# Moving value products, projections and squares by a step or two in a fused attention and feed-forward kernel

## Chip, cores and metric

The kernel runs on one core of one Trainium2 chip, in one launch. The metric is the device time of that launch in microseconds (us). A core has TensorE (PE, with its weight loads shown as PEld), VectorE (DVE), ScalarE (ACT), GpSimd (POOL), and SyncE (SP), which issues the DMAs here. Each engine executes its own instructions in order and waits on semaphores.

## What is computed

A pre-normalized attention block and a gated feed-forward, both with a residual, on 2048 tokens of width 512 with 32 heads of 16:

```python
def _A_ref(x, wqkv, wo):                       # S=2048, D=512, H=32, Dh=16
    qkv = (x @ wqkv).reshape(B, S, 3, H, Dh).transpose(2, 0, 3, 1, 4)
    q, k, v = qkv[0], qkv[1], qkv[2]
    p = _softmax(jnp.einsum("bhqd,bhkd->bhqk", q, k) * (Dh ** -0.5), axis=-1)
    o = jnp.einsum("bhqk,bhkd->bhqd", p, v)
    return o.transpose(0, 2, 1, 3).reshape(B, S, D) @ wo

def _B_ref(x, w_gate, w_up, w_down):           # F=1792
    return (_gelu(x @ w_gate) * (x @ w_up)) @ w_down

h = x + _A_ref(_layernorm(x), A_wqkv, A_wo)
h2 = h + _B_ref(_layernorm(h), B_w_gate, B_w_up, B_w_down)
```

Inputs and output are bfloat16. There is no causal mask; the softmax subtracts the maximum of each row.

## The kernel before

**Units and steps.** The 2048 queries are cut into 8 groups of 256, and the 32 heads into 8 slots of 4. One (group, slot) is a unit; there are 64, in the order of the groups. The main loop (`while True`, L1403) runs in steps (`tick`); a unit has 16 steps.

**First pass.** In a step TensorE computes two 128x512 score tiles (`p1_pair`, L825) and VectorE takes their row maxima in one instruction (`p1_consume`, L840). After 16 steps GpSimd combines the maxima of the unit (`negm_part`, `negm_pre`), writes them with corrections into `ST`, SP transposes `ST` into `STG`, and GpSimd adds that to the query tile (L888), so that the second pass subtracts the maximum inside the matmul.

**Second pass.** It runs `P2_START` = 24 steps behind the first. In a step TensorE computes two transposed score tiles (`p2_tile`, L904) and ScalarE turns each into probabilities (`p2_consume`, L933), which go to a ring of 34 tiles in `PTM`, `PTE` and `PTG`.

**Eleven joint units.** In the units of `JOINT` one step of the first pass is left out (step 14). Two differences of score tiles (`item_diff`, L1022 and L1024 on TensorE, L1027 on ScalarE) are made ahead, and VectorE folds them in at step 10 or 11 (L837). ScalarE makes up its two tiles in the steps that follow.

**Dense work.** Everything else on TensorE is done in items, generators that give out a piece per step: projections of queries, keys and values, value products (`item_pv`, L947, 64 products of a unit in four pieces), the output projection (`item_oproj`, L1087 and L1091), gate and up products (`item_gate`, `item_up`, L1168), down products (`item_down`, L1220). `Dense.piece` holds three lists: `prio` (value products and output projections, ordered by the step before which they may not start), `extra` (differences) and `ready` (all else). An item of `ready` starts only if it ends before the next item of `prio` may start. Steps without a piece get dummy products (`dummy`, L1380). The dense item and the second pass share four PSUM banks.

**Account of ScalarE.** `act_lag` estimates how far ScalarE is behind: an exponential adds 0.478, an eviction 0.48, a step takes off 1.135. Gate and up products start only at a lag of at most `LAG_START` = 0.3, squares are written at a lag of at most `LAG_OP` = 0.2, tanh at `LAG_TH`, differences at `LAG_EXTRA`; otherwise they are put off by a step (`defer`). A difference is forced from the second step of its own unit.

**The chain behind a value product.** When the four pieces are done, ScalarE evicts the sum to `OB` (L669). SP transposes it to `OBT` (`o_turn`, L973). Five steps later GpSimd gets the reciprocal (L981) and the scaling into `Otok` (L985). When all 8 slots of a group are there, `post_onT` loads the residual (`load_xres`, L1060) and transposes `Otok` into `OnT` (L1067), through `clear`, which lets such a transfer out only at certain steps of a unit. It then adds the two output projections to `prio`. After a projection, ScalarE evicts with a sum (L1094), then squares with a sum (`sq`, L1101); GpSimd normalizes (L1111 to L1125), and `post_hnT` transposes into `hnT_l` (L1077, again through `clear`). Some steps after the second of these, `add_ffn_when` adds the group's feed-forward to `ready`: 7 gate and 7 up items and 2 down items, with a chain of multiplications on GpSimd and a tanh on ScalarE (L1148) for each gate item.

**The tail.** After the last maximum the second pass goes on alone for 24 steps with wide exponentials (L921), VectorE evicts in ScalarE's place (L658), and the feed-forward of the last group follows.

Of the kernel before, what the change touches and what calls it, by code (L numbers as in the profile page):

```python
# [218 lines left out]

NPT_M, NPT_E, NPT_G = 23, 4, 7  # L220
NPT = NPT_M + NPT_E + NPT_G
PV_T = (13, 14, 16, 17)
ADDX = 3
LAGX = 8
PAUSE = 1
# [4 lines left out]
LAG_OP = 0.2  # L230
# [1 line left out]
SLOPE = 0.02  # L232
JOINT = (12, 14, 17, 20, 25, 28, 33, 36, 41, 44, 49)
J_AT, J_GONE = 10, 14
LAG_EXTRA = 0.2
POLY = 1.3
TICK = 1.135
TOOK = {1.04: 1.13, 0.62: 0.7, 1.27: 1.26, 1.45: 1.67, 0.31: 0.4}
# [3 lines left out]
def bass_sequential_preLN__mha_block__geglu_ffn__prompt_kernel(nc, A_x, A_wqkv, A_wo, B_x, B_w_gate, B_w_up, B_w_down, out):  # L242
    dbg = None
    with ExitStack() as es:
# [279 lines left out]
        class Dense:  # L524
# [27 lines left out]
            def piece(self):  # L552
                if self.single and self.pause > 0:
                    return 0
                while True:
                    if self.gen is None:
# [6 lines left out]
                        elif self.prio and (not self.single or self.prio[0][3] <= self.now):  # L563
                            self._start(self.prio.pop(0))
                        elif self.extra and not tight() and act_lag[0] <= LAG_EXTRA and self.now + 2 <= lim and not (self.ready and self.ready[0][0] is item_up):
                            self._start(self.extra.pop(0))
# [26 lines left out]
        dense = Dense()  # L593
        behind = [0]
        def tight():
            return dense.now // 16 in JOINT and dense.now % 16 >= J_GONE - 2 or bool(behind[0])

        deferred = []
        def defer(k, fn):
            deferred.append((dense.now + k, fn))  # L600
        force = [False]
# [47 lines left out]
        act_lag = [0.0]  # L649
        def act_more(cost):  # L650
            act_lag[0] += cost
# [4 lines left out]
        def evac_act(o_ap, i_ap, reads, writes, scale=None, extra=(), bias=None, then=None, cost=0.48):  # L656
            if dve_free[0] and scale is None and bias is None:
                P.op("dve", lambda e: e.tensor_copy(out=o_ap, in_=i_ap), reads=reads, writes=writes, extra_deps=extra)  # L658
                if then is not None:
                    then()  # L660
                return
            act_more(cost)
            kw = {}
            if scale is not None:
                kw["scale"] = scale
            if bias is not None:
                P.op("act", lambda e: e.activation(out=o_ap, in_=i_ap, func=ACT.Identity, bias=bias, **kw), reads=list(reads) + ["kbias"], writes=writes, extra_deps=extra)
            else:
                P.op("act", lambda e: e.activation(out=o_ap, in_=i_ap, func=ACT.Copy, **kw), reads=reads, writes=writes, extra_deps=extra)  # L669
            if then is not None:  # L670
                then()
# [264 lines left out]
        def item_pv(b, ui):  # L936

            gi, slot = units[ui]
            for p in range(4):
                while not force[0] and dense.now < P2_START + 16 * ui + 4 * p + 5:  # L940
                    yield ("wait", 1)
                for m in (2 * p, 2 * p + 1):
                    for i in range(2):
                        kt = 2 * m + i
                        for g in range(4):
                            pi = pt_of[(ui, m, g)]
                            P.op("pe", lambda e, g=g, kt=kt, pi=pi, i=i: e.matmul(pbank[32 * g:32 * g + 17, b, 0:256], VA[:, kt, 4 * slot + g, :],  # L947
                                                                                  PTt(pi)[:, 256 * i:256 * i + 256], start=(kt == 0), stop=(kt == NT - 1), tile_position=(0, 32 * g)),
                                 reads=[("V", kt), "VA_ones", ("PT", pi)], writes=[("pb", b)], sig=(g == 3 and i == 1))
                    for g in range(4):  # L950
                        pt_busy.discard(pt_of.pop((ui, m, g)))
                if p < 3:
                    yield 2
            par, col = slot // 2 % 2, slot % 2
            if gi == GL and slot >= NSLOT - 2:
                evac_act(OA[:, par, 256 * col:256 * col + 256], pbank[:, b, 0:256], [("pb", b)], [("OA", par, col), ("RB", 1)], cost=0.27)
                if col == 0:
                    dense.add(item_ofin, gi, front=True, est=3, not_before=dense.now + 3)
            else:
                evac_act(OB[:, ui % 2, :], pbank[:, b, 0:256], [("pb", b)], [("OB", ui % 2)], cost=0.27, then=lambda: o_turn(ui))  # L960
            pv_done.add(ui)
            return 2

        pv_done = set()
        P2_START = 16 + LAGX

        ob_busy = {}
        def o_turn(ui):
            gi, slot = units[ui]
            par = ui % 2  # L970
            assert not ob_busy.get(par), "GpSimd too far behind"
            ob_busy[par] = True
            P.dma("sp", lambda e: e.dma_start_transpose(out=OBT[:, par, :, :], in_=OB[:, par, :]), ("obT", par), reads=[("OB", par)], writes=[("OBT", par)])  # L973
            o4 = OBT[:, par].rearrange("p q (g i) -> p q g i", i=32)
            defer(5, lambda: o_norm(gi, slot, par, o4, ("OBT", par), ob_busy))
# [25 lines left out]
            yield  # L1001

        def clear(fn):
            if not force[0] and not 5 <= dense.now % 16 <= 14:
                defer(1, lambda: clear(fn))
            else:
                fn()
# [36 lines left out]
        def add_ffn(gi):  # L1044
            for f in range(NFC // 2):
                dense.add(item_gate, gi, f, est=3)
                dense.add(item_up, gi, f, est=3)
            for k in range(2):
                dense.add(item_down, gi, k, est=5)

        def add_ffn_when(gi):
            if w_pieces or not qkv_over[0]:
                defer(1, lambda: add_ffn_when(gi))
            else:
                add_ffn(gi)

        def load_xres(gi):
            assert gi < 2 or ffn_done.get(gi - 2), "dense stream too far behind (residual reuse)"
            for k in range(2):
                P.dma("sp", lambda e, k=k: e.dma_start(out=g_h(gi, k), in_=xv[:, 2 * gi + k, :]), ("xres", gi % 2, k), writes=[("h", gi % 2, k)])  # L1060

        otok_consumed = {}
        def post_onT(gi, k):
            gp = gi % 2
            if k == 0:
                load_xres(gi)
            P.dma("sp", lambda e: e.dma_start_transpose(out=OnT[:, k, :, :], in_=Otok[:, k, :]),  # L1067
                  ("onT", k), reads=[("Otok", s_) for s_ in range(NSLOT)], writes=[("OH", k)])
            if k == 1:
                otok_consumed[gi] = True  # L1070
            dense.add(item_oproj, gi, k, front=True, est=3, not_before=dense.now + 4)

        hn_left = {}
        ffn_done = {}
        def post_hnT(gi, k):
            gp = gi % 2
            P.dma("sp", lambda e: e.dma_start_transpose(out=hnT_l[gp][:, :, 128 * k:128 * k + 128], in_=hn_sb[:, k, :]),  # L1077
                  ("hnT", 2 * gp + k), reads=[("OH", k)], writes=[("hnT", gp, k)])
            hn_left[gi] = hn_left.get(gi, 2) - 1
            if hn_left[gi] == 0:  # L1080
                defer(3, lambda: add_ffn_when(gi))

        def item_oproj(b, gi, k):
            gp, t = gi % 2, 2 * gi + k
            hh = g_h(gi, k)
            for hc in range(4):
                P.op("pe", lambda e, hc=hc: e.matmul(pbank[:, b, :], OnT[:, k, hc, :], wo_sb[:, hc, :], start=(hc == 0), stop=False),  # L1087
                     reads=[("OH", k), "wo"], writes=[("pb", b)], sig=False)
                if hc == 1:
                    yield 2  # L1090
            P.op("pe", lambda e: e.matmul(pbank[:, b, :], ident[:], hh, start=False, stop=True),  # L1091
                 reads=["ident", ("h", gp, k)], writes=[("pb", b)], sig=True)
            act_more(0.48)
            P.op("act", lambda e: e.activation(out=hh, in_=pbank[:, b, :], func=ACT.Copy, accum_out=hsum[:, t:t + 1]),  # L1094
                 reads=[("pb", b)], writes=[("h", gp, k), ("hsum", t)])
            def sq():
                if not force[0] and act_lag[0] > LAG_OP:
                    defer(1, sq)
                    return
                act_more(0.48)  # L1100
                P.op("act", lambda e: e.activation(out=hn_sb[:, k, :], in_=hh, func=ACT.Square, accum_out=hsq[:, t:t + 1]),  # L1101
                     reads=[("h", gp, k)], writes=[("OH", k), ("hsq", t)])
                defer(1, lambda: pool.add(ln2_from_sums(gi, k, t), then=lambda: defer(2, lambda: clear(lambda: post_hnT(gi, k)))))
            defer(2, sq)
            return 3
# [297 lines left out]
        while True:  # L1403
# [71 lines left out]
            if p2_ok and t2 % 16 == 0:  # L1475
                dense.add(item_pv, t2 // 16, front=True, est=5, not_before=tick + PV_T[0])
            if doubles[0]:
# [61 lines left out]
```

## Time and profile before

| | |
|---|---|
| median of 3 runs | 1240.03 us (1239.23 to 1241.87) |
| profiled execution | 1240.23 us, span 1238.5 us |
| VectorE busy | 1182.2 us (95%) |
| ScalarE busy | 1196.3 us (97%) |
| TensorE busy | 1099.2 us (89%), of it 206.0 us dummies (L1380) |
| GpSimd busy | 785.3 us (63%) |
| row maxima L840 | 1002, 1141.9 us |
| first maximum starts, last one ends | 14.73 us, 1183.08 us |
| squares L1101 | 14 |
| transposes OnT<-Otok, hnT_l<-OnT | 14 each, 2.7 and 2.6 us to landing in the median |
| granted TensorE clock | full, but for two spells of 3.4 us at half (from 820.4 and 1090.1 us) |

Times within the profile count from the start of the span. A row of a group names line, engine and operation, what is written and read, the count, then busy time and the mean of one in ns, then the idle time of that engine just before the group and what ended it. A row of a timeline has start, duration, engine, line, operation and count, and in brackets the idle time before it. A row of a stretch has its bounds, its length, the busy time (and number of instructions) of PE, PEld, DVE, ACT and POOL, the granted TensorE clock, the share of the DMA engines and GB/s.

### The profile page before, as it was taken

The numbers are of one execution on the slowest core, as the hardware profiler recorded it, in microseconds if no ns is written. First come the engines' busy times: TensorE is split into PE (matmuls) and PEld (weight loads), VectorE is DVE, ScalarE is ACT, GpSimd is POOL, SyncE is SP. The second block draws the span as 40 slices with busy tenths as digits, with TensorE's granted clock in tenths as the row PEclk, the third lists the DMA queues.
The fourth block names the chain that finished last, engine by engine and source line by source line (L and its number), as shares of the span: only waits on it lengthen the run. The fifth ranks groups of instructions, "written<-read, shape, count | busy, mean of one in ns | idle before, by whom it ended". The sixth has DMA issues, their size and how long they took to land.

```text
span 1238.5 us, 31200 instructions
## 1 busy us (share of the span) xinstructions
PE 1099.2 (89%) x12389; PEld 429.3 (35%) x12588; DVE 1182.2 (95%) x1111; ACT 1196.3 (97%) x2433; POOL 785.3 (63%) x1624
## 2 busy tenths in 40 slices
PE   7898888888888999889988999989988898888888
PEld 3232222233333333333333333333333333323345
DVE  8999999999999999999999999999999999999933
ACT  7899999999999999999999999999999999999992
POOL 8555884455756467674667638574676847865781
PEclk9999999999999999999999999999999999999999
DMA  5111113400010001000010100100001000010000
GB/s 151 27 30 25 30 27 108 117 10 8 10 25 17 14 12 23 16 15 17 8 27 12 14 17 8 27 16 15 12 10 30 12 18 8 7 32 20 8 15 18
DMA packets 68656, 31.52 MB, mean 25 GB/s; under 512 B 53920, under 2 KB 67488, under 8 KB 68512
## 3 DMA queue, kind: packets, MB, share of 16 engines
q1 hardware_dynamic: 68512, 29.52, 9.9%
q8 instruction: 101, 1.65, 0.6%
q14 instruction: 43, 0.35, 0.1%
HBM read 11.80 MB, written 2.10 MB: 11 GB/s over the span
## 4 chain that ended last, share of the span: by engine, by line
ACT 59%; DVE 30%; PE 8%; issue 1%; POOL 1%; DMA 1%
ACT PTM L933 33%; DVE PM L840 29%; ACT PTG L933 10%; ACT PTE L933 6%; PE pbank L1220 2%; ACT th_sb L1148 2%; ACT u_sb L669 2%; ACT g_sb L669 1%; PE pbank L825 1%; ACT PTM L921 1%; PE pbank L904 1%; PE pbank L1380 1%; PE pbank L1168 1%; ACT OB L669 1%; ACT OnT L1101 1%
## 5 line engine op out<-in xcount | busy, mean ns | idle before, releaser
L840 DVE TENSOR_REDUCE PM<-pbank 128x2 f32<-128x1024 f32 x1002 | 1141.9, 1213 | 11.3 <-PE pbank L904 7.4
L933 ACT ACTIVATE PTM<-pbank 128x512 bf16<-128x512 f32 x1357 | 727.4, 704 | 6.6 <-PE pbank L904 2.0
L904 PE MATMUL pbank<-QT,KT 32*128 32x256 bf16 x4096 | 517.6, 273 | 17.8 <-ACT PTM L933 6.5
L825 PE MATMUL pbank<-KT,QT 32*128 32x512 bf16 x2026 | 390.5, 384 | 25.3 <-DVE PM L840 10.7
L1380 PE MATMUL pbank<-ones_bf,ident 128*128 128x512 bf16 x639 | 206.0, 384 | 65.0 <-ACT PTM L933 31.9
L933 ACT ACTIVATE PTG<-pbank 128x512 bf16<-128x512 f32 x407 | 227.6, 704 | 1.2
L825 PEld LDWEIGHTS pbank<-KT,QT 32*128 32x128 bf16 x2026 | 98.7, 91 | 367.6 <-DVE PM L840 134.4
L904 PEld LDWEIGHTS pbank<-QT,KT 32*128 32x128 bf16 x4096 | 171.5, 92 | 90.4 <-ACT PTM L933 47.2
L933 ACT ACTIVATE PTE<-pbank 128x512 bf16<-128x512 f32 x236 | 137.3, 700 | 0.6
L947 PE MATMUL pbank<-PTM,VA 128*17 128x256 bf16 x2776 | 126.0, 274 | 5.2 <-ACT PTG L933 1.1
L981 POOL TENSOR_TENSOR LINV<-OBT,negone 128x8 f32<-128x8 bf16 x62 | 103.4, 1667 | 0.0
L1380 PEld LDWEIGHTS pbank<-ones_bf,ident 128*128 128x128 bf16 x804 | 46.2, 97 | 137.4 <-ACT PTM L933 90.8
L947 PEld LDWEIGHTS pbank<-PTM,VA 128*17 128x17 bf16 x2776 | 59.9, 89 | 49.7 <-issue 29.8
L1158 POOL TENSOR_TENSOR th_sb<-g_sb 128x512 f32<-128x512 f32 x49 | 50.9, 1039 | 34.9 <-ACT g_sb L669 34.9
L868 POOL TENSOR_TENSOR MX<-PM,MX 128x8 f32<-128x8 f32 x64 | 12.8, 200 | 92.7 <-DVE PM L840 92.1
L1168 PE MATMUL pbank<-hnT_l,wg_sb 128*128 128x256 bf16 x448 | 66.6, 274 | 2.8 <-ACT PTG L933 0.2
L1168 PE MATMUL pbank<-hnT_l,wu_sb 128*128 128x256 bf16 x448 | 66.5, 275 | 2.8 <-ACT PTM L933 0.2
L888 POOL TENSOR_TENSOR QT<-QT,STG 128x256 bf16<-128x256 bf16 x64 | 42.7, 668 | 35.0 <-DMA STG<-ST 35.0
L1157 POOL TENSOR_TENSOR th_sb<-th_sb,g_sb 128x512 f32<-128x512 f32 x49 | 62.1, 1267 | 3.2
L1160 POOL TENSOR_TENSOR th_sb<-th_sb,g_sb 128x512 f32<-128x512 f32 x49 | 62.1, 1267 | 2.9
L1212 POOL TENSOR_TENSOR GUT<-th_sb,u_sb 128x512 bf16<-128x512 f32 x49 | 62.1, 1267 | 2.0
L855 POOL TENSOR_TENSOR MX<-PM,MX 128x8 f32<-128x8 f32 x64 | 12.9, 201 | 74.8 <-DVE PM L840 74.0
(164 smaller groups left out, 1138.6 us busy)
## 6 DMA issues: line engine op xcount, KB each, us to landing
QKS<-QKS SPq DMA_DIRECT2D x27, 112.0 KB, 2.1
x_sb<-in_A_x_dram SPq DMA_DIRECT2D x4, 512.0 KB, 5.6
xres<-in_A_x_dram SPq DMA_DIRECT2D x16, 128.0 KB, 2.3
out_dram<-out_sb SPq DMA_DIRECT2D x16, 128.0 KB, 1.7
wg_sb<-in_B_w_gate_dram SPq DMA_DIRECT2D x4, 448.0 KB, 4.0
wu_sb<-in_B_w_up_dram SPq DMA_DIRECT2D x4, 448.0 KB, 3.9
wd_sb<-in_B_w_down_dram SPq DMA_DIRECT2D x3, 512.0 KB, 5.0
STG<-ST SPq DMA_TRANSPOSE x64, 2.3
```

Source lines behind the costliest of these rows:

```text
L825: P.op("pe", lambda e, g=g, b=b: e.matmul(pbank[:, b, :], QT[32 * g:32 * g + 32, c, slot, 128 * qt:128 * qt + 128], KT[32 * g:32 * g + 32, ...
L840: P.op("dve", lambda e: e.tensor_reduce(out=PM[:, par, qt, kc, g:g + 2], in_=pbank[:, b:b + 2, :], axis=AX.X, op=ALU.max), reads=[("pb", b ...
L904: P.op("pe", lambda e, kt=kt, i=i: e.matmul(pbank[:, b, 256 * i:256 * i + 256], KT[32 * g:32 * g + 32, slot, 128 * kt:128 * kt + 128], QT[ ...
L933: P.op("act", lambda e, b=b, pi=pi: e.activation(out=PTt(pi), in_=pbank[:, b, :], func=ACT.Exp), reads=[("pb", b)], writes=[("PT", pi)], e ...
L947: P.op("pe", lambda e, g=g, kt=kt, pi=pi, i=i: e.matmul(pbank[32 * g:32 * g + 17, b, 0:256], VA[:, kt, 4 * slot + g, :], PTt(pi)[:, 256 * ...
L981: P.op("pool", lambda e: e.tensor_tensor(out=li, in0=o4[:, :, :, 16], in1=negone[:, 0:8].rearrange("p (q h) -> p q h", q=2), op=ALU.pow), ...
L1157: o(1.27, lambda e: e.tensor_tensor(out=ts_, in0=ts_, in1=gs, op=ALU.mult), [("th", par), ("g", par)])], then=done)
L1158: pool.add([o(1.04, lambda e: e.tensor_tensor(out=ts_, in0=gs, in1=gs, op=ALU.mult), [("g", par)], dE), o(0.62, lambda e: e.tensor_scalar( ...
L1160: o(1.27, lambda e: e.tensor_tensor(out=ts_, in0=ts_, in1=gs, op=ALU.mult), [("th", par), ("g", par)])], then=poly_done)
L1168: P.op("pe", lambda e, dc=dc, fc=fc, i=i: e.matmul(pbank[:, b, 256 * i:256 * i + 256], w[:, dc, 128 * fc:128 * fc + 128], hT[:, dc, :], st ...
L1212: P.op("pool", lambda e: e.tensor_tensor(out=o_ap, in0=shp(ts_), in1=shp(us), op=ALU.mult), reads=[("th", par), ("u", par)], writes=o_keys ...
L1380: P.op("pe", lambda e: e.matmul(pbank[:, b, :], ident[:], ones_bf[:, 0:512], start=True, stop=True), reads=["ident", "ones_bf"], writes=[( ...
```

## The change

Six places of the order are changed; no computation is.

- The four pieces of a unit's value products may start at steps 15, 16, 17 and 18 after the unit's second pass began. Before, the first could start at step 13 and the loop's own condition was 4p + 5 for piece p.
- A difference may be taken early at a lag of 0.3 instead of 0.2.
- `clear` lets transfers out at steps 5 to 13 of a unit instead of 5 to 14.
- The output projection starts at the earliest 5 steps behind its transfer instead of 4.
- The feed-forward is added 4 steps behind its second transfer instead of 3.
- A square counts 0.48 more lag while a gate or up product is running.

```diff
-PV_T = (13, 14, 16, 17)
+PV_T = (15, 16, 17, 18)
...
-LAG_EXTRA = 0.2
+LAG_EXTRA = 0.3
...
             for p in range(4):
-                while not force[0] and dense.now < P2_START + 16 * ui + 4 * p + 5:
+                while not force[0] and dense.now < P2_START + 16 * ui + PV_T[p]:
                     yield ("wait", 1)
...
         def clear(fn):
-            if not force[0] and not 5 <= dense.now % 16 <= 14:
+            if not force[0] and not 5 <= dense.now % 16 <= 13:
                 defer(1, lambda: clear(fn))
...
-            dense.add(item_oproj, gi, k, front=True, est=3, not_before=dense.now + 4)
+            dense.add(item_oproj, gi, k, front=True, est=3, not_before=dense.now + 5)
...
             if hn_left[gi] == 0:
-                defer(3, lambda: add_ffn_when(gi))
+                defer(4, lambda: add_ffn_when(gi))
...
             def sq():
-                if not force[0] and act_lag[0] > LAG_OP:
+                if not force[0] and act_lag[0] + (0.48 if dense.gen is not None and dense.cur in (item_gate, item_up) else 0) > LAG_OP:
                     defer(1, sq)
                     return
```

The main loop, which the diff does not touch, adds a unit's value products with `not_before=tick + PV_T[0]` (L1476).

## The prediction

> **What bounds the kernel now.** I read the page first (busy times, chain, costliest groups), then the waits of VectorE, then the timeline of ScalarE and VectorE around the waits, then of TensorE and the DMA queue, then busy times by stretch.
>
> ```profile
> span 1238.5 us, 31200 instructions
> ...
> PE 1099.2 (89%) x12389; PEld 429.3 (35%) x12588; DVE 1182.2 (95%) x1111; ACT 1196.3 (97%) x2433; POOL 785.3 (63%) x1624
> ...
> ACT 59%; DVE 30%; PE 8%; issue 1%; POOL 1%; DMA 1%
> ...
> L840 DVE TENSOR_REDUCE PM<-pbank 128x2 f32<-128x1024 f32 x1002 | 1141.9, 1213 | 11.3 <-PE pbank L904 7.4
> ```
>
> The row maxima (L840) set the length: 1002 of them fill 1141.9 of 1238.5 us with only 11.3 us of idle before them. What the change can win in the main stage is what VectorE idles there:
>
> ```profile
> DVE PM L840 <- PE pbank L904: 7.4, 23, 1.1
> ```
>
> One maximum lasts 1.21 us, but 16 undisturbed ones start within 18.10 us, 1.13 apart, so every gap also loses an overlap of 0.08: 7.4 + 23 x 0.08 = 9.2 us is the ceiling. All 23 waits are for TensorE, which executes in order and is itself held up by ScalarE (no free bank) or by a DMA. ScalarE's view:
>
> ```profile
> 815.86 0.82 ACT L1101 ACTIVATE OnT<-xres 128x512 bf16<-128x512 bf16 x1
> 816.38 0.39 ACT L1101 ACTIVATION_READ_ACCUMULATOR OnT<-xres 128x1 f32 x1
> 816.47 1.27 ACT L933 ACTIVATE PTM<-pbank 128x512 bf16<-128x512 f32 x2
> 817.42 0.81 ACT L669 ACTIVATE u_sb<-pbank 128x512 f32<-128x512 f32 x1
> 817.90 2.29 ACT L933 ACTIVATE PTM<-pbank 128x512 bf16<-128x512 f32 x4
> 819.80 0.88 ACT L1027 ACTIVATE OA<-pbank 128x512 f32<-128x512 f32 x1
> ```
>
> From start to start an exponential or an eviction takes 0.48 us, a square (L1101 with its accumulator read) 0.61. A step of 1.13 needs two exponentials, 0.96, so only 0.17 to 0.18 us per step is left for all else. Here a square, an eviction and a difference (1.57 us) fall into four steps that hold 0.7. VectorE just behind:
>
> ```profile
> 818.77 2.35 DVE L840 TENSOR_REDUCE PM<-pbank 128x2 f32<-128x1024 f32 x2 [0.20 <-PE pbank L904]
> 821.72 1.22 DVE L840 TENSOR_REDUCE PM<-pbank 128x2 f32<-128x1024 f32 x1 [0.60 <-PE pbank L904]
> 823.23 3.56 DVE L840 TENSOR_REDUCE PM<-pbank 128x2 f32<-128x1024 f32 x3 [0.29 <-PE pbank L904]
> ```
>
> The other large wait is a transposing transfer that an output projection waits for. It goes out behind another transpose and the residual load:
>
> ```profile
> 1082.86 1.17 SPq L973 DMA_TRANSPOSE OBT<-OB  x1
> 1084.08 1.05 SPq L1060 DMA_DIRECT2D xres<-in_A_x_dram  x2
> 1085.17 3.38 SPq L1067 DMA_TRANSPOSE OnT<-Otok  x2
> ```
>
> ```profile
> 1088.53 0.60 PE L1087 MATMUL pbank<-wo_sb,OnT 128*128 128x512 bf16 x2 [1.75 <-DMA OnT<-Otok]
> ```
>
> Behind it TensorE runs at half clock for 3.4 us, as it does at 820.4:
>
> ```profile
> 820.43:823.85 3.42, 3.09 (x31) 0.82 (x30) 2.53 (x3) 2.89 (x7) 2.32 (x7) 0.50 0.09 19
> ...
> 1086.70:1090.10 3.40, 1.65 (x15) 0.45 (x11) 2.33 (x3) 2.09 (x6) 2.51 (x6) 1.00 0.39 80
> 1090.10:1093.50 3.40, 3.40 (x18) 0.74 (x17) 2.99 (x3) 3.16 (x8) 2.24 (x8) 0.50 0.01 2
> ```
>
> **Part by part.** No instruction is added or removed; all is order. The sum goes against the profiled execution's own 1240.23 us (span 1238.5 and 1.7 around it); the median of the runs, 1240.03, is 0.2 lower.
>
> *Squares.* Of the 14 squares, five share a step with a running gate or up product in the order of before: those at 525.44, 670.65, 815.86, 946.39 and 958.19. Each is followed 1.56 us later by the eviction of that product. Idle of VectorE behind them: 0.21, 0.21, 0.20 + 0.60 + 0.29, 0.46, 0.17: 2.14 us in seven gaps, and 7 x 0.08 = 0.56 of lost overlap, 2.7 together. The new condition adds 0.48 to the account of ScalarE's lag while such a product runs, so a square stays back until there is room. It is not lost: 0.61 us is worked off in steps whose account is empty. What it delays is normalization on GpSimd and the transpose into hnT_l; in all four groups concerned the feed-forward of the group before still runs for some 35 to 43 steps, so nobody waits for that. I take 2.3 of the 2.7, since the difference behind three of them (L1027, forced at the second step of its unit) stays unless the larger LAG_EXTRA places it earlier. Bounds: +0.5 (a held square meets another activation) to -2.7.
>
> *Projection one step later.* Only one of the 14 transfers was waited for. It cost VectorE 1.07, then 0.34 and 0.46 at half clock: 1.87, with three overlaps 2.1. One step is 1.13 of TensorE's 1.75 us wait. But the value products end one step later as well, and their eviction and transpose (L973) stand ahead of this transfer on the queue: if they stay ahead, transfer and projection move together and nothing is gained. If the transfer goes out first, as in the other groups, all of 2.1 goes. Bounds 0 to -2.1; I take -1.4, nearer to the second, because six groups of seven stand that way.
>
> *Value products at 15, 16, 17, 18 of their unit instead of 13, 14, 15, 17* (the old loop's condition 4p+5 binds only the last). Four pieces without the empty step between: dense work gets one more step in sixteen. TensorE pays nothing, since a piece of 16 products replaces dummies of the same 0.43 us; the covering dummies are L1380's 206 us. On TensorE's queue the pieces stand behind the exponentials that they read; one or two steps more relieve waits of L947 (5.2, 1.6 and 0.7 us of idle by operand), which lie only partly on the path. Probability tiles are freed up to two steps later: the ring of 34 refills the first of them at step 17, products at 15, so ScalarE does not wait. The eviction (OB) and its transpose go out one step later; SP waits there for ScalarE, and what stands behind it on SP is at most an OnT or hnT_l transpose and, six steps on, STG. GpSimd's reciprocal runs at the unit's end in both orders, with one step less of cover; its queue idles 35.0 us before L888 as it is. Estimate from the gaps of 0.17 to 0.33 that recur beside these products (486 to 526 us): -0.5, bounds -2.3 to +2.3, as they may vanish or double.
>
> *Window 5 to 13 and feed-forward 4 steps behind.* No transpose of before goes out at step 14, and no gate product waits for its transfer: 0. For the last group the delays add up to two or three steps, 2.3 to 3.4 us, before its feed-forward; its last up product ends at 1201.9 while the last value products begin at 1202.64, and these move two short steps of 0.92 as well: 0, bounds 0 to +2.1 (two groups of 1.05 on TensorE behind the loop).
>
> *Tail.* Two of the last four pieces move behind the last exponentials. TensorE has 0.25 + 0.72 idle there and a piece is 0.43: +0.2, bounds 0 to +0.9.
>
> Sum: -2.3 - 1.4 - 0.5 + 0 + 0.2 = -4.0: 1236.2 for the profiled execution, 1236.0 for the median.
>
> The clock enters two of these terms. The half-clock spell follows a window of 3.4 us in which TensorE was busy 1.65 us, with no single gap above 1.75; before 820.43 the gaps were shorter still. So here a light window is enough, and with the waits the spells should go: the -4.0 counts on that.
>
> The Trainium skill (TensorE: Matmul & The Clock Gate, "Why this matters for your kernels") asks for no idle gap above about 3 us if the clock is not to drop; by that rule neither of these waits causes its spell, the spells would stay, and the sum would be -2.0 instead.
>
> **Rivals.**
> 1. *ScalarE overfilled (slower).* With one more step for dense work a unit can carry four gate, up or projection evictions instead of three. A unit with at most six activations beside its exponentials takes 18.10 us; those of 488 to 507 and 507 to 526 with seven and eight take 18.89 and 18.76. At 0.7 each, twelve more such units cost 8.4: 1236.0 + 8.4 = 1244.4. It decides from the seventh activation on, and from more than six such units the kernel is slower. Against: the planner charges 0.478 per exponential and 0.48 per eviction, as measured, and starts no gate or up product above a lag of 0.3.
> 2. *Only reshuffled: the change doesn't do what it says.* The held squares and differences meet other activations, and the transfer still goes behind L973. With +0.5 and 0 in place of -2.3 and -1.4 the sum is +0.2: 1240.2. For: the projection's transfer and the value products move by the same step.
> 3. *Half-clock spells recur.* If two windows stay light, their part stays: 0.60 + 0.29 + 0.34 + 0.46 and four overlaps, 2.0: 1238.0. For: the window before 820.4 has no long wait in it. Against: all other windows of the main stage keep full clock.
> The rule of the Trainium skill quoted above gives this time too.
> 4. *The repeated gaps go too.* With feed-forward further ahead at each group's boundary most of the ceiling of 9.2 is won: 1232. For: the gaps near 497, 505 and 516 return in three groups. Against: nothing in the change aims at them.
> 5. *Tail.* The last gate and up fall behind the last value products: 2.1 more on the path, 1238.1.
>
> **How the numbers follow.** Forecast 0.42, rival 1 0.15, rival 2 0.13, rival 3 0.08, rival 4 0.16, rival 5 0.06. A measurement here can tell 0.2%, 2.5 us, from no change. Faster by more than that (below 1237.6): forecast, rival 4, and half of 3 and 5, 0.65. Same: 2 and the other halves, 0.20. Slower (above 1242.5): 0.15. The range goes from 1230, just beyond the ceiling, to 1243.5, into rival 1; the forecast's own is 1233.5 to 1238.
>
> **What would show it.** Right: no square within two microseconds ahead of an eviction of g_sb or u_sb; VectorE's waits for L904 down from 7.4 to about 4.5 us; no wait of L1087 for OnT; OBT's transposes one step later against the maxima. Wrong: L840's idle at or above 11.3, units of 18.7 us and more in greater number, half-clock spells at new places, or more than 55.4 us behind the last maximum.

## Result and the profile after

The changed kernel takes 1234.78 us in the median of five runs (1234.71 to 1235.26) against 1240.03: a ratio of 0.9954, 95% interval 0.9943 to 0.9966. The forecast was 1236.0. The profiled execution takes 1234.76 us (span 1232.9).

Of the page of the changed kernel, the span, the busy times and the group of the row maxima:

```profile
span 1232.9 us, 31298 instructions
...
PE 1102.3 (89%) x12444; PEld 427.4 (35%) x12580; DVE 1179.1 (96%) x1107; ACT 1195.2 (97%) x2437; POOL 784.4 (64%) x1624
...
L840 DVE TENSOR_REDUCE PM<-pbank 128x2 f32<-128x1024 f32 x1002 | 1141.4, 1213 | 8.8 <-PE pbank L904 5.1
```

The maxima do the same work in the same time, with 2.5 us less idle before them. In the waits of VectorE (total, times, longest):

```profile
DVE PM L840 <- PE pbank L904: 5.1, 20, 0.4
```

The longest of them is 0.4 instead of 1.1 us. The DMA queue and TensorE at the last two transposes into OnT:

```profile
1074.57 1.05 SPq L1060 DMA_DIRECT2D xres<-in_A_x_dram  x2
1075.66 2.50 SPq L1067 DMA_TRANSPOSE OnT<-Otok  x2
1083.44 1.17 SPq L973 DMA_TRANSPOSE OBT<-OB  x1
```

```profile
1083.50 0.38 PE L1087 MATMUL pbank<-wo_sb,OnT 128*128 128x512 bf16 x1 [0.38 <-ACT OB L669]
```

The transposes into OnT go out ahead of the transpose into OBT, not behind it, and 7 steps ahead of the projection, which now waits 0.38 us for a bank and not 1.75 us for a DMA. The granted clock is full in this main stage.

The span is 5.6 us shorter, and it splits otherwise than forecast: the last maximum ends at 1180.48 instead of 1183.08 us (-2.6), and 52.44 us lie behind it instead of 55.43 (-3.0).

To place the gain within the main stage, the starts of the maxima in the profiled executions are set against undisturbed steps (1.13 us each), and what VectorE loses is summed over eight units each, in us:

| kernel | 0-7 | 8-15 | 16-23 | 24-31 | 32-39 | 40-47 | 48-55 | 56-63 |
|---|---|---|---|---|---|---|---|---|
| before | 5.4 | 0.5 | 1.1 | 2.0 | 2.0 | 3.0 | 1.2 | 3.5 |
| after | 5.6 | 1.0 | 2.0 | 2.2 | 1.8 | 1.8 | 1.3 | 0.6 |
| value products alone | 5.6 | 1.7 | 3.3 | 2.1 | 4.0 | 2.1 | 1.9 | 0.6 |
| after without LAG_EXTRA | 5.6 | 1.0 | 2.4 | 2.0 | 3.6 | 2.1 | 1.7 | 0.6 |

The gain lies in the last column (2.9: the OnT wait and its spell at half clock) and in units 40 to 47 (1.2). Most of this 1.2 is the other spell of the profiled execution, from 820.43 us: units 28, 36 and 44 of the kernel before have the same order, square, eviction and difference included, and lose 0.3, 0.3 and 1.2 us; only in the third does the clock drop. In units 8 to 23 about 1.4 is lost.

### The profile page after: what moved, and what is told of

It reads as the page before. It is cut to its first block, busy times and chain, and to the rows that moved or that the text cites. A ratio compares the mean times of both kernels' runs of the same rounds, so it can differ in the third digit from the quotient of the medians.

```text
span 1232.9 us, 31298 instructions
## 1 busy us (share of the span) xinstructions
PE 1102.3 (89%) x12444; PEld 427.4 (35%) x12580; DVE 1179.1 (96%) x1107; ACT 1195.2 (97%) x2437; POOL 784.4 (64%) x1624
## 4 chain that ended last, share of the span: by engine, by line
ACT 50%; DVE 30%; POOL 8%; PE 7%; issue 3%; DMA 1%; POOLq 0%; DVEq 0%
DVE PM L840 29%; ACT PTM L933 29%; ACT PTG L933 8%; ACT PTE L933 4%; PE pbank L1220 2%; ACT g_sb L669 1%; POOL th_sb L1158 1%; PE pbank L904 1%; ACT u_sb L669 1%; DMA STG<-ST 1%; PE pbank L825 1%; ACT th_sb L1148 1%; POOL LINV L981 1%; PE pbank L1168 1%; POOL GUT L1212 1%
## 5 line engine op out<-in xcount | busy, mean ns | idle before, releaser
L904 PE MATMUL pbank<-QT,KT 32*128 32x256 bf16 x4096 | 512.2, 273 | 16.2 <-ACT PTM L933 6.0
L1380 PE MATMUL pbank<-ones_bf,ident 128*128 128x512 bf16 x697 | 217.3, 383 | 56.2 <-ACT PTM L933 29.1
L904 PEld LDWEIGHTS pbank<-QT,KT 32*128 32x128 bf16 x4096 | 171.2, 92 | 85.2 <-ACT PTM L933 46.5
L1168 PE MATMUL pbank<-hnT_l,wg_sb 128*128 128x256 bf16 x448 | 67.0, 275 | 3.6
L1168 PE MATMUL pbank<-hnT_l,wu_sb 128*128 128x256 bf16 x448 | 67.1, 275 | 2.3
L868 POOL TENSOR_TENSOR MX<-PM,MX 128x8 f32<-128x8 f32 x64 | 12.8, 200 | 86.6 <-DVE PM L840 86.3
L1220 PE MATMUL pbank<-wd_sb,GUT 128*128 128x512 bf16 x210 | 57.3, 382 | 3.4 <-ACT OB L669 1.3
```

Source lines behind the costliest of these rows:

```text
L904: P.op("pe", lambda e, kt=kt, i=i: e.matmul(pbank[:, b, 256 * i:256 * i + 256], KT[32 * g:32 * g + 32, slot, 128 * kt:128 * kt + 128], QT[ ...
L1168: P.op("pe", lambda e, dc=dc, fc=fc, i=i: e.matmul(pbank[:, b, 256 * i:256 * i + 256], w[:, dc, 128 * fc:128 * fc + 128], hT[:, dc, :], st ...
L1220: P.op("pe", lambda e: e.matmul(pbank[:, b, :], GUT[:, fc, 128 * k:128 * k + 128], wd_sb[:, fc, :], start=first, stop=last), reads=[("GUT" ...
L1380: P.op("pe", lambda e: e.matmul(pbank[:, b, :], ident[:], ones_bf[:, 0:512], start=True, stop=True), reads=["ident", "ones_bf"], writes=[( ...
```

## Experiments

**The value products alone, and the squares alone.** First the value products, with nothing else of the change:

```diff
-PV_T = (13, 14, 16, 17)
+PV_T = (15, 16, 17, 18)
...
-                while not force[0] and dense.now < P2_START + 16 * ui + 4 * p + 5:
+                while not force[0] and dense.now < P2_START + 16 * ui + PV_T[p]:
```

> The kernel before with the value products' new steps alone. Freed-step theory (four pieces without the empty step leave dense work one step more in each unit, the feed-forward runs ahead, and with it go the squares beside gates, the forced differences, the awaited transfer and part of the tail): 1234.8 us, within 1 of the whole change; squares within 2 us ahead of an eviction of g_sb or u_sb 0 instead of 5, less than 53.5 us behind the last maximum. Rival as the prediction had it (squares' condition 2.3, projection 1.4, value products 0.5): 1239.5, with 55.4 us behind the last maximum.

Measured: 1239.85 us, ratio 0.9995 (0.9987 to 1.0004). The tail is 52.44 us as in the whole change, but the last maximum ends at 1185.60, 2.5 us later than before. The projection of unit 34 waits:

```profile
651.99 0.38 PE L1087 MATMUL pbank<-wo_sb,OnT 128*128 128x512 bf16 x1 [2.24 <-DMA OnT<-Otok]
```

and two spells of half clock begin at 278.03 and 332.64 us. So this part wins 3.0 us in the tail and loses 2.5 in the main stage. The freed-step theory's 1234.8 was missed; the rival's 1239.5 comes near, but not for its reason, since it left the tail at 55.4.

The squares' condition alone:

```diff
-                if not force[0] and act_lag[0] > LAG_OP:
+                if not force[0] and act_lag[0] + (0.48 if dense.gen is not None and dense.cur in (item_gate, item_up) else 0) > LAG_OP:
```

> The kernel before with the squares' condition alone. Both theories let the idle of VectorE behind the five squares go: 1237.7 (1240.0 less 2.3), between 1237.2 and 1238.7, the wait for OnT near 1085 and 55.4 us behind the last maximum unchanged. If the squares only meet other activations instead: 1240.

Measured: 1240.95 us, ratio 1.0009 (1.0000 to 1.0018), last maximum at 1183.34, tail 55.42. It wins nothing; both theories had 1237.7. The condition does move the squares: the next eviction of g_sb or u_sb now follows 4.7 us or more behind each, where it followed 1.56 us behind five of them. But units 28 and 36 lose 0.3 us each as before. In unit 28 the kernel before has this gap, 2.9 us behind the square:

```profile
528.35 9.33 DVE L840 TENSOR_REDUCE PM<-pbank 128x2 f32<-128x1024 f32 x8 [0.21 <-PE pbank L904]
```

With the condition it is gone, but a tanh (L1148) stands 3.9 us earlier in the unit than before, and 2.8 us behind it there is another:

```profile
532.21 0.92 ACT L1148 ACTIVATE th_sb<-th_sb 128x512 f32<-128x512 f32 x1
```

```profile
534.97 3.49 DVE L840 TENSOR_REDUCE PM<-pbank 128x2 f32<-128x1024 f32 x3 [0.18 <-PE pbank L904]
```

**Everything but the value products.** The changed kernel with this part undone, the other five edits kept:

```diff
-PV_T = (15, 16, 17, 18)
+PV_T = (13, 14, 16, 17)
...
-                while not force[0] and dense.now < P2_START + 16 * ui + PV_T[p]:
+                while not force[0] and dense.now < P2_START + 16 * ui + 4 * p + 5:
```

> The whole change without the value products' new steps. Freed-step theory: dense work has no more room than before and differences and projections are shifted in it, nine or more gate and up products of the last group fall behind the last maximum: 1240 or more, over 56 us behind the last maximum. Rival (squares' condition and projection carry the gain): 1236.5 (1240.0 less 2.3 and 1.4, plus 0.2).

Measured: 1266.49 us, ratio 1.0215 (1.0201 to 1.0229). The main stage is the shortest of all (last maximum at 1178.40), and 85.8 us lie behind it: feed-forward that the main stage left over. The kernel before has the value products at these same steps and a tail of 55.43 us, so the other five edits without them put off 30 us of work; which of the five does it is not isolated.

**With a hole between the pieces:**

```diff
-PV_T = (13, 14, 16, 17)
+PV_T = (15, 16, 17, 19)
...
-                while not force[0] and dense.now < P2_START + 16 * ui + 4 * p + 5:
+                while not force[0] and dense.now < P2_START + 16 * ui + PV_T[p]:
```

> The kernel before with value products at steps 15, 16, 17 and 19: two steps later, the empty step kept. Freed-step theory: no dense step is won, 1239 or more, over 55 us behind the last maximum. Rival (later start, so that TensorE waits less for probabilities): 1235 to 1236, as the whole change.

Measured: 1250.97 us, ratio 1.0088 (1.0074 to 1.0102), last maximum at 1179.09, tail 69.9 us. One empty step between the pieces, with the later place kept, costs 17.5 us of tail against the closed-up order. It is not the hole by itself: the kernel before has one too, between steps 15 and 17, and a tail of only 55.43. Why the hole costs more at the later place is not isolated.

**Closed up without the later place:**

```diff
-PV_T = (13, 14, 16, 17)
+PV_T = (14, 15, 16, 17)
...
-                while not force[0] and dense.now < P2_START + 16 * ui + 4 * p + 5:
+                while not force[0] and dense.now < P2_START + 16 * ui + PV_T[p]:
```

> The kernel before, with the value products at steps 14, 15, 16 and 17 of their unit: four consecutive steps as in the change, but ending where the old ones ended. Closing-up theory: what shortens the tail is the step freed for dense work, not the later place; feed-forward of the last full group ends at step 1022 here too, so the tail takes 52.2 to 52.8 us as in the change, and 69.9 with the hole is not seen. Rival, later-place theory: reading the probabilities two steps later is what relieves the end; the tail stays at 54.5 to 55.5. Main stage: with four steps before the projection's release unchanged and the pieces ending a step earlier, the wait for OnT goes where it was in value products alone by the transfer theory (last maximum at 1181 to 1183, 1235 to 1237.5 in all); if waits do not decide it, the main stage is as in value products alone (1185.6, 1239.9).

Measured: 1234.81 us, ratio 0.9954 (0.9942 to 0.9967), tail 52.46, last maximum at 1181.43. With nothing else changed it is as fast as the whole change. For the tail the freed step is what counts; "two steps later" isn't needed for it.

**What in the leftover sets the tail.** The changed kernel with the last full group's feed-forward 16 steps later:

```diff
-                defer(4, lambda: add_ffn_when(gi))
+                defer(4 + 16 * (gi == GL - 1), lambda: add_ffn_when(gi))
```

> The changed kernel, with the feed-forward of the last full group released 16 steps later and nothing else touched: its last up product moves from step 1022 to 1041, so that one gate and one up product, and three tanh instead of one, fall behind the last maximum (5 such products before, 9 with the hole, 12 without the later value products). Leftover theory: the tail is set by how much feed-forward is left over; at 0.6 us for each product (55.43 - 52.44 over five) up to 2 us, the tail takes 53.5 to 56 and the kernel 1236 to 1238.5. Rival: the tail is shorter because the last value products themselves stand otherwise; it stays at 52.2 to 52.8 and the kernel at 1234.8. The main stage ends at 1180.5 +- 0.4 by both.

Measured: 1237.84 us, ratio 0.9981 (0.9972 to 0.9990), tail 55.43 us: exactly that of before, although only two gate and up products are left over and not five. So the price isn't 0.6 us for each product. TensorE's timeline of the changed kernel, its down products (L1220) and the last group's projection (L1262):

```profile
1194.40 0.59 PE L1220 MATMUL pbank<-wd_sb,GUT 128*128 128x512 bf16 x2
...
1195.80 1.47 PE L1220 MATMUL pbank<-wd_sb,GUT 128*128 128x512 bf16 x6
1197.70 1.25 PE L1220 MATMUL pbank<-wd_sb,GUT 128*128 128x512 bf16 x5
...
1204.35 0.59 PE L1262 MATMUL pbank<-wo_sb,OnT 128*128 128x512 bf16 x2 [0.16 <-issue]
1205.21 0.81 PE L1262 MATMUL pbank<-wo_sb,OnT 128*128 128x512 bf16 x3
1206.19 0.81 PE L1220 MATMUL pbank<-wd_sb,GUT 128*128 128x512 bf16 x3
1207.27 2.54 PE L1220 MATMUL pbank<-wd_sb,GUT 128*128 128x512 bf16 x11
```

and of ffn_held, with the tanh (L1148) in ScalarE's timeline below it:

```profile
1205.91 0.59 PE L1262 MATMUL pbank<-wo_sb,OnT 128*128 128x512 bf16 x2 [0.16 <-issue]
1206.78 0.81 PE L1262 MATMUL pbank<-wo_sb,OnT 128*128 128x512 bf16 x3
1207.76 0.81 PE L1220 MATMUL pbank<-wd_sb,GUT 128*128 128x512 bf16 x3
1208.84 2.54 PE L1220 MATMUL pbank<-wd_sb,GUT 128*128 128x512 bf16 x11
1211.42 0.81 PE L1220 MATMUL pbank<-wd_sb,GUT 128*128 128x512 bf16 x3
```

```profile
1204.99 0.82 ACT L1148 ACTIVATE th_sb<-th_sb 128x512 f32<-128x512 f32 x1
```

In the changed kernel one of the two down items runs between the last exponentials, on time that TensorE has; only the other stands behind the projection. In ffn_held and before, the last tanh starts 23.4 us behind the last maximum (2.35 in the changed kernel), the down products need it, and both items stand behind the projection: 14 products more at some 0.22 us, the 3.0 us. Later tanh go with longer tails: 40 us behind the last maximum with the hole (69.9), 54 without the value products (85.8).

**Which edit mends the main stage.** The whole change, once without the projection's fifth step and once without the larger LAG_EXTRA:

```diff
-            dense.add(item_oproj, gi, k, front=True, est=3, not_before=dense.now + 5)
+            dense.add(item_oproj, gi, k, front=True, est=3, not_before=dense.now + 4)
```

> The changed kernel with one part undone: the projection may again start 4 steps behind the issue of its transposing transfer, as before. Against value products alone (1239.85) the whole change gains 5.1 us, all of it in the main stage (last maximum at 1180.48 instead of 1185.60, with the same 52.44 behind it). Transfer theory: those 5.1 us are the projection's waits for OnT (2.24 and 0.79 us in value products alone) and what follows them (half-clock spells, gaps of VectorE); the fifth step cures them. Then this kernel waits for OnT again by over 0.5 us in some group, its last maximum lies at 1183 to 1186, and it takes 1237.5 to 1240. Rival, difference theory: LAG_EXTRA of 0.3 places the extra differences so that no unit is overfilled, and the projection's step is worth little; then the last maximum lies below 1181.5 and the kernel takes 1234.5 to 1236. Both expect 52.4 us behind the last maximum, since feed-forward ends at step 1022 in this order too.

Measured: 1233.82 us, ratio 0.9946 (0.9932 to 0.9959), last maximum at 1179.51, no wait for OnT.

```diff
-LAG_EXTRA = 0.3
+LAG_EXTRA = 0.2
```

> The changed kernel with LAG_EXTRA back at 0.2 and all the rest kept. Transfer theory: the projection's fifth step is there, no wait for OnT over 0.5 us, so the last maximum lies at 1180 to 1181.5 and the kernel takes 1234.5 to 1236. Difference theory: the extra differences stand as in value products alone, so the units with gaps of 0.7 to 2.1 us (14, 16, 17, 34) are back; the last maximum lies at 1183.5 to 1186, the kernel takes 1237.5 to 1240. 52.4 us behind the last maximum by both.

Measured: 1240.08 us, ratio 0.9996 (0.9987 to 1.0005). The profiled execution is its quickest (1237.65; last maximum at 1183.48, tail 52.44). The prediction's reason for the fifth step falls: the fifth step is there, and the projection of unit 34 still waits 1.91 us. What stands ahead of its transfer shows on SP's queue, in no_ex:

```profile
638.03 1.17 SPq L882 DMA_TRANSPOSE STG<-ST  x1
644.30 0.35 SPq L1240 DMA_DIRECT2D out_dram<-out_sb  x1
644.69 0.92 SPq L1060 DMA_DIRECT2D xres<-in_A_x_dram  x2
645.65 2.93 SPq L1067 DMA_TRANSPOSE OnT<-Otok  x2
```

```profile
650.09 0.38 PE L1087 MATMUL pbank<-wo_sb,OnT 128*128 128x512 bf16 x1 [1.91 <-DMA OnT<-Otok]
```

The store of a first output half (L1240) is at the head of the queue from 639.2 to 644.3, waiting 5.1 us for ScalarE's eviction of out_sb, and residual and transposes wait behind it though their data are there. With a LAG_EXTRA of 0.3 a difference starts at step 2 of units 26, 34 and 42, the down item that started there goes to step 0 of the next unit, and its store no longer meets the transposes.

**The store alone.** no_ex, with that store queued behind the transposes and the order of all other engines as it was:

```diff
-            P.dma("sp", lambda e: e.dma_start(out=outv[:, t, :], in_=out_sb[:, oi, :]), ("out", oi), reads=[("osb", oi)], writes=[("outd", t)])
+            store = lambda: P.dma("sp", lambda e: e.dma_start(out=outv[:, t, :], in_=out_sb[:, oi, :]), ("out", oi), reads=[("osb", oi)], writes=[("outd", t)]); defer(4, store) if k == 0 and gi < GL - 1 else store()
```

> The kernel of no_ex (LAG_EXTRA 0.2, the rest of the change kept; 1240.08 us) with one thing altered: the store of a group's first output half (L1240) is queued four steps later, so that on SP's queue it stands behind the transposes into OnT (L1067) instead of ahead of them. All other engines' orders are the same. In no_ex that store stands at the head of SP's queue from 493.9 to 499.0 us, waiting 5.1 us for ScalarE to evict out_sb, and both OnT transposes go out at step 8 of units 26, 34, 42 instead of step 3; the projection of unit 34 then waits 1.91 us. Queue theory: this is the larger part of what LAG_EXTRA is worth, since a difference placed at step 2 puts the first down product off past the projection. Then OnT goes out at step 3 or 4 in units 26, 34 and 42, no wait over 0.5 us is left, unit 34 loses 1.3 us or more, the half-clock share of the executions shrinks, and the kernel takes 1235.5 to 1238. Difference theory: where the differences stand is what costs (VectorE's gaps of 0.74 us in units 16, 30, 38, 46 against 0.31); then only unit 34 gains, and the kernel takes 1238.5 to 1240. Between 1238 and 1238.5 neither alone.

Measured: 1237.80 us, ratio 0.9968 (0.9958 to 0.9979). SP's queue and the projection:

```profile
639.83 1.17 SPq L882 DMA_TRANSPOSE STG<-ST  x1
641.05 1.05 SPq L1060 DMA_DIRECT2D xres<-in_A_x_dram  x2
642.14 2.50 SPq L1067 DMA_TRANSPOSE OnT<-Otok  x2
650.31 1.17 SPq L973 DMA_TRANSPOSE OBT<-OB  x1
651.52 0.58 SPq L1240 DMA_DIRECT2D out_dram<-out_sb  x1
```

```profile
650.37 0.38 PE L1087 MATMUL pbank<-wo_sb,OnT 128*128 128x512 bf16 x1 [0.40 <-ACT OB L669]
```

OnT goes out five steps earlier and the wait is gone; units 28 to 36 take 145.29 us instead of 146.80. Of LAG_EXTRA's 5.3 us (1240.08 to 1234.78) the store accounts for 2.3 by the medians; by the ratios it is 0.0028, 3.5 us. The other 2 to 3 us are not isolated. Some 0.35 us in each group of eight units from 20 to 52 lies between the profiles of this kernel and of the change (differences at other steps); and the executions of this kernel have a mean clock of 0.997 to 1.000, those of the change 1.000 throughout. At a mean clock of 1.000 there are one execution of no_ex (1237.65 us), three of this kernel (1236.24, 1236.29 and 1237.28) and five of the change (1234.71 to 1235.26). So at equal clock LAG_EXTRA is worth some 2.9 us, the store about half of it (1.5 us in unit 34 by the profiles), and the rest of the 5.3 goes with spells of half clock that the change does not have.

**Only the two parts.** The kernel before with:

```diff
-PV_T = (13, 14, 16, 17)
+PV_T = (15, 16, 17, 18)
...
-LAG_EXTRA = 0.2
+LAG_EXTRA = 0.3
...
-                while not force[0] and dense.now < P2_START + 16 * ui + 4 * p + 5:
+                while not force[0] and dense.now < P2_START + 16 * ui + PV_T[p]:
```

> The kernel before with two parts of the change: value products at steps 15 to 18 and LAG_EXTRA 0.3; projection, feed-forward, window and squares as before. Theory now held: these two carry all of the gain; value products alone gave the tail of 52.44 us, LAG_EXTRA gives the main stage (no output store ahead of OnT on SP's queue), and the other four edits give nothing or less (the fifth step of the projection cost 1.0 us: 1233.82 without it). Then 1233.4 to 1234.4 us, last maximum at 1179.2 to 1180, 52.4 behind it. Rival: the later feed-forward transposes or the held squares matter after all; then 1235 to 1237.

Measured: 1233.55 us (1233.47 to 1233.87), ratio 0.9938 (0.9923 to 0.9953), last maximum at 1179.39, tail 52.44, the fastest kernel of the study. VectorE idles 8.8 us before its maxima, as in the change.

**Closed up and LAG_EXTRA, without and with the fifth step.** The closed-up kernel with the first of these lines, then with both:

```diff
-LAG_EXTRA = 0.2
+LAG_EXTRA = 0.3
...
-            dense.add(item_oproj, gi, k, front=True, est=3, not_before=dense.now + 4)
+            dense.add(item_oproj, gi, k, front=True, est=3, not_before=dense.now + 5)
```

> A candidate: the kernel before with the value products at 14, 15, 16, 17 and LAG_EXTRA 0.3, nothing else. Closed up alone took 1234.81 with its last maximum at 1181.43, two half-clock spells among them (units 11 and 14: 1.31 and 1.10 us). Theory: LAG_EXTRA again places differences ahead of the first down product, the gaps of units 11, 14 and 16 (1.3, 1.1, 0.7) go at least in half, and nothing is won in the tail: 1232.8 to 1234.2. Rival: in this order no store stood ahead of OnT but in units 34 and 50, so LAG_EXTRA only moves gaps about: 1234.3 to 1236.

> The same candidate with the projection's fifth step added. In the change that step cost about 1 us (1234.78 with it, 1233.82 without). If it costs by itself, by putting dense work off once in each group, this kernel is 0.5 to 1.5 us slower than closed_up_ex; if it cost only through where the first down product and its store then stood on SP's queue, the two are within 0.4 us of each other or this one is faster.

Measured: 1236.21 us, ratio 0.9962 (0.9950 to 0.9974), and 1234.82, ratio 0.9945 (0.9930 to 0.9960). The first misses both its ranges: 1.4 slower than closed up alone, though no store stands ahead of OnT in it. The two profiles don't settle why: that of closed up alone is its one execution with spells of half clock (1235.94), and even so units 12 to 60 take 869.4 us there and 869.3 here. Why the two edits do not add up stays open. The second is as fast as closed up alone: the fifth step saves 1.4 us here, while in the change it costs about 1.0 (by the medians; the two ratios' intervals overlap). Most of the 1.4 can be placed. In the first kernel the first gate product of a group (L1168) waits 1.98 us in unit 11: its transposing transfer into hnT_l stands behind a load of down weights (L696) on SP's queue and lands at 237.41, 0.06 us before the product's weights are loaded. The unit loses 1.6 us. With the fifth step the transfer has landed 0.9 us ahead of the product, nothing waits, and the unit loses 0.4. By itself the step has no fixed price.

## Why the prediction was right, and where its steps failed

The total held, 1.2 us from the forecast, but of its five terms only one (window and feed-forward, 0) stands as it was put, and the edit that decides the main stage had no term of its own.

- **Squares, -2.3: wrong in its mechanism and credited to the wrong edit.** Alone the condition gains nothing (1240.95), although it moves the squares as the prediction said. The first step that failed is that the room a held square leaves stays free: a tanh moves into it and opens a gap of about the same size (0.18 for 0.21 us). Of the 2.14 us of idle that the term was taken from, 0.60 and 0.29 lie within the spell at 820.43 and are not in units 28 and 36, where the order is the same. In the change the condition has nothing to hold back: the order of every engine is the same without it, and the same with the window of 5 to 14. The squares do stand free of gate and up products, as forecast, because the value products' freed step lets the last up product of each of the first seven groups come 20 to 76 steps earlier. The second step that failed is the reading of the order of before as given: five squares were counted beside gate and up products without asking whether another edit of the same change moves those products away. The losses behind them in units 36 and 44 (0.3 and 1.2 us) are gone.
- **Projection, -1.4 with bounds of 0 and -2.1: right place, wrong cause.** The wait of 1.75 us and its half clock are gone, worth 2.9 us in units 56 to 63. But that column reads 0.6 with value products alone too, where the projection stands 4 steps behind. The case that the prediction took as the nearer one, the transfer ahead of L973, happened through the value products.
- **Value products, -0.5 with bounds of -2.3 and +2.3.** Alone +2.5 in the main stage, just beyond the upper bound. The prediction followed this edit on SP's queue only to the OBT transposes and what stands behind them; that earlier down products bring their output store ahead of OnT, where it waits 5.1 us, was not seen.
- **LAG_EXTRA had no term**, only half a sentence under the squares (a forced difference may be placed earlier). It is worth 5.3 us here (and costs 1.4 in the closed-up kernel), and without it the change would have measured as no change: rival 2's 1240.2, by another mechanism.
- **Tail, +0.2 with bounds of 0 and +0.9: -3.0.** Mis-sized with the wrong sign. The prediction counted the two pieces that move behind the exponentials, and saw that the last up product ended at 1201.9, but not that the down products behind it could come free early enough to run under the exponentials.
- **Window and feed-forward 4 steps behind, 0: right for this order.** Without them, the squares' condition and the fifth step, pv_ex stays within 0.3 us of no_op, which has all but the fifth step. (In closed_up_ex a gate product does wait for its transfer, as shown above.)
- **Rivals.** The start of rival 1 is seen: new gaps of 0.4 and 0.2 us at steps 9 and 10 of units 16, 17, 30, 31, 38, 39, 46 and 47, 2.8 us behind a tanh that fell beside value products; together they are 2.5 of the 8.8 us of idle that remain. Where twelve units of 18.8 us and more were priced, one came (unit 19, 19.0); of 18.7 and more there are 6 behind the first unit, before 11. Rivals 3 and 5 did not come; of rival 4's repeated gaps, some went and others came.
- **What it said would show it.** No square within two microseconds ahead of an eviction of g_sb or u_sb, and no wait of a projection for OnT: both seen, both with another cause. The transposes into OBT do go out one step later (10.8 instead of 9.8 steps behind the start of their unit, where nothing is in the way). VectorE's waits for L904 fell to 5.1, not 4.5. That the sum came out near rests on two errors of opposite sign: 1.6 too much in the main stage, 3.2 too little in the tail.

The clock: the prediction counted on light windows as the cause of the half-clock spells. The runs don't bear that out: windows as light keep full clock, and most spells follow busy ones (last section). The rule of the Trainium skill that it set beside it (TensorE: Matmul & The Clock Gate, "Why this matters for your kernels": no idle gap above about 3 us) doesn't describe these spells either: the longest gaps in the window ahead of each of ten of them are 0.10 to 1.85 us.

## What to carry to other kernels

Where a planner writes the order, an edit's effect is the order that comes out: run the parts singly and ask of each which others it moves, for here one condition had no effect beside another edit, and a lag threshold was worth 5.3 us, about 2.3 of it through a store that it moved on a queue. On a queue that executes in order, look at what waits at its head, not only at the transfer that is late; a store with no hurry can hold up a transfer that TensorE needs. In a tail, ask which work still fits under the last long stage: one tanh that came 21 us later cost 3.0 us, whether five products were left or two.

## What the runs showed of the hardware

- Spells of half clock (3.4 us, in two of the kernels once or twice 6.8) also come without any long wait. In ten stretches of 3.41 us ahead of such a spell, in six kernels, TensorE was busy 1.56 to 1.72 us in three (longest gap 1.50 to 1.85) and 2.78 to 3.14 us in seven (longest gap 0.10 to 0.33). In the execution of value products alone, a stretch with 1.50 us and a gap of 1.90 (most of the 2.24 us for which the projection of unit 34 waits) is followed by full clock. It starts on the grid of the spells (next point), 109.0 times 3.413 us behind 278.03. The rows have stretch, length, TensorE busy and so on, with the granted clock third from the end:

```profile
650.08:653.49 3.41, 1.50 (x14) 0.56 (x17) 1.85 (x2) 1.69 (x4) 0.88 (x4) 1.00 0.41 61
```

  while this one of the same execution is followed by half clock:

```profile
329.22:332.64 3.42, 3.03 (x25) 1.15 (x26) 3.42 (x4) 3.42 (x9) 2.96 (x8) 1.00 0.08 16
332.64:336.05 3.41, 3.10 (x17) 0.58 (x18) 2.54 (x3) 2.76 (x6) 3.33 (x5) 0.50 0.02 3
```

  So neither the busy share nor the longest gap that the profile shows tells which stretch is followed by half clock; the cause stays open.
- The spells of one execution lie on a grid: 278.03 and 332.64 are 16.0 times 3.413 us apart, 820.43 and 1090.09 in the kernel before 79.0 times.
- The spread between executions goes with the clock. Value products alone: 1237.5 and 1238.5 us at a mean clock of 1.000, 1239.1 to 1241.6 at 0.995 to 0.997, 1242.1 at 0.994. The kernels that keep it at 1.000 spread over less than 0.6 us (the change, no_op, pv_ex). Seven executions of the kernel before at a mean clock of 1.000 lie at 1238.6 to 1239.2 us. So at equal clock the change is worth some 4 of its 5.3 us; the rest is spells of half clock that its executions do not have. Why this order has none is not shown.
